# Fourier mixing with a gated MLP: forms made in place, a product begun on a copy, weights split earlier

## The chip, the cores and the metric

The kernel runs on one core of a Trainium2 chip. The metric is the device time of one execution in microseconds. Its engines are TensorE (PE, matrix products, results in PSUM), VectorE (DVE) and ScalarE (ACT, both elementwise), GpSimd (POOL) and SyncE (SP); the last two issue most of the DMA transfers here.

## The reference

Shapes: x is 2048 x 512 (one batch), the sequence matrices are 2048 x 2048, the hidden ones 512 x 512, w1 and w3 are 512 x 1376, w2 is 1376 x 512; all are float32.

```python
a = einsum("bsd,ed->bse", x, dft_hid_re)
b = einsum("bsd,ed->bse", x, dft_hid_im)
y = einsum("ts,bse->bte", dft_seq_re, a) - einsum("ts,bse->bte", dft_seq_im, b)

h = silu(x @ w1) * (x @ w3)
o = h @ w2

g = sigmoid((x * gate_w).sum(-1, keepdims=True))
return g * y + (1 - g) * o
```

## The kernel before, in words

**Arithmetic.** Each float32 operand is split in two: a high half, made by ScalarE's copy into the matrix format (`zh`, `f1P`, `wa` and so on), and a low half, made by VectorE's subtraction of the high half from the source (`split`, lines 70 to 74). One product is then three matmuls (`mm3`, line 81: high with high, high with low, low with high). A 2 x 2 block product is computed by seven block products instead of eight, in the manner of Strassen and Winograd. They are named P1 to P7, and their operands are blocks or sums of blocks ("forms").

**Stages.** First come the hidden-dimension products (14 of them, tiles `dP`), whose results go to the scratch `ab` in HBM. Then eleven items, one for each chunk `c` of 128 columns of w1 and w3 (`item(c)`, products into the banks `X`, `Z`, `Y`, `Yi`), which write h to the scratch `hsp` and `hpl`. Then six blocks 0 to 5: for `m` = 0 (h times w2), 1 (real part) and 2 (imaginary part), and two halves of the rows each. Blocks 0 to 3 go through P1, P5, P6, P3, P7, P2, P4 in this order; blocks 4 and 5 have no P2 of their own, but an inner set of seven smaller products (`Lx`). A product has three steps in blocks 0 and 1 (quarters `q` = 0 to 2, and a short "plain" step after P3, P7, P2 and P4), and four in blocks 2 to 5. `STEPS` lists all the steps, and `AT[b, k, q]` is the number of one of them. Block 0 is steps 0 to 24, block 1 begins at step 25.

**The stationary forms.** `forms(m, q, ks, keep)` loads a quarter of `ab` (two tiles `r`) or of w2, makes the sums that the products in `ks` need (tiles `m..P`), splits each, and either keeps the result in SBUF (`keep` true: in place, a tile of the pool `op`) or stores it in the scratch `fsp` (`keep` false), from where `load_a` fetches it when its block draws near (tiles `a0P`, `a1P`, `a2P`). It returns a list of functions, one for the loads and one for each product. `inner_forms` does the same for the inner set, and its stores go to `lsp`. The functions with `keep` false, and the inner ones, stand in the list `later`; `work(n)` takes `n` of them. Twelve are taken in the hidden stage, and six in each item (hooks `h0` to `h4`). Those with `keep` true stand in `TASKS`, a table of what is done after a given step.

**The moving forms.** For step `n`, `load_c` fetches a raw block up to eight steps ahead (tiles `B`), `sum_c` adds blocks four steps ahead (line 669), and `split_c` splits three steps ahead (tiles `zh` and `zl`, from a pool of eight).

**PSUM.** Four pairs of banks, with the tags 0 to 3. P1 opens pair 1 or 0, P5 pair 2, P2 pair 3; P6, P7 and P4 go on accumulating on P1's, and P3 on P5's. After P1, P5 and P6 ScalarE copies the pair to SBUF (line 906), and VectorE adds the later product to that copy (line 911), after which `finish` scales and stores it. In the items, pairs 0 and 1 are `X`, pair 2 is `Y` and `Yi`, and pair 3 is `Z`.

**What sets the order.** A planner puts the instructions of every engine into a queue of their own at compile time. It follows the order of the program, but takes a later instruction first where, by its own estimate of durations, that one is ready sooner. An instruction passed to `pinned` stays behind what its engine had before it. On the chip each queue runs strictly in the order so made.

**The start of the items.** `begun(0)` lets ScalarE copy `X` into `Y` (line 358), so that `Y` goes on from there. The parts of `second(0, ...)` follow in the order 0, 3, 1, 4, 2, 5, and part 3 is `begun`. After them `prep_wa(1)` splits chunk 1's weights (`wa`, on lines 71 and 74), which item 0 uses in `first1(1)`.

Of the kernel before, what the change touches and what calls it, by code (L numbers as in the profile page):

```python
# [9 lines left out]
AF = mybir.ActivationFunctionType  # L10
# [18 lines left out]
def fnet_swiglu_gate_kernel(  # L29
# [17 lines left out]
    nc = tc.nc  # L47
# [8 lines left out]
    def pair(k, name):  # L56
        return psum.tile([P, 2, 512], F32, tag=f"pp{k}", name=name)

    def raw(name, n=1024):
        return f4.tile([P, n], F32, tag="f4", name=name)  # L60

    def half(ap, n=2):
        return ap.rearrange("p (a n) -> p a n", a=n)

    def flat(ap):
        return ap.rearrange("p a n -> p (a n)")

    pinned = tc.keep_in_program_order

    def split(hi, lo, src, pin=False):  # L70
        i = nc.scalar.activation(hi, src, AF.Copy)  # L71
        if pin:
            pinned(i)
        nc.vector.tensor_sub(lo, src, hi.bitcast(F32))  # L74
# [177 lines left out]
    def prep_wa(c):  # L252
        n = 768 if c == NC - 1 else 512
        if n == 512:
            t = zo.tile([P, 2, n], F32R, tag="zo", name=f"wa{c}")
            h, l = t[:, 0], t[:, 1]
        else:
            h, l = (zo.tile([P, n], F32R, tag="zo", name=f"wa{c}{v}") for v in "hl")
        split(h, l, WS[c][:, :n], c == 1)
        WA[c] = half(h, n // 256), half(l, n // 256)  # L260
# [201 lines left out]
    def rows_of(m, q):  # L462
        if m == 0:
            return [w2[h, q] for h in range(2)]
        return [ab[m - 1, g, q].rearrange("p h i e -> p (h i e)") for g in range(2)]

    def width(m, q):
        return 256 if m == 0 and 2 * q + 1 == NP else 512
# [4 lines left out]
    def forms(m, q, ks, keep):  # L473

        n = width(m, q)
        st = {}

        def load():
            for h, src in enumerate(rows_of(m, q)):
                st[h] = raw(f"r{m}{q}{h}")  # L480
                nc.sync.dma_start(st[h][:, : 2 * n], src[:, : 2 * n])
            st["a11"], st["a21"] = (st[0][:, v * n : (v + 1) * n] for v in range(2))
            st["a12"], st["a22"] = (st[1][:, v * n : (v + 1) * n] for v in range(2))

        def total(k):
            if k in ("P5", "P3") or k == "P7" and "m" not in st:
                st["m"] = raw(f"m{m}{q}{k}")
            if k == "P5":
                src = st["m"][:, :n]
                nc.vector.tensor_sub(src, st["a22"], st["a21"])  # L490
                st["s5"] = src
            elif k == "P6":
                src = st["m"][:, n : 2 * n]
                minus_sum(src, st["s5"], st["a11"])
                st["s6"] = src
            elif k == "P3":
                src = st["m"][:, :n]
                minus_sum(src, st["a12"], st["s6"])
            elif k == "P7":
                src = st["m"][:, n : 2 * n]  # L500
                nc.vector.tensor_sub(src, st["a11"], st["a21"])
            else:
                src = st[{"P1": "a11", "P2": "a12", "P4": "a22"}[k]]
            st[k] = src

        def parts(k):
            src = st[k]
            pool, tag = (op, "op") if keep else (f4, "f4")
            t = pool.tile([P, 2, n], F32R, tag=tag, name=f"f{m}{k}{q}")
            split(t[:, 0], t[:, 1], src)  # L510
            if keep:
                A[m, k, q] = t
            else:
                nc.gpsimd.dma_start(fsp[m, PRODS.index(k), q, :, : 2 * n], flat(t.bitcast(F32)))

        return ahead(load, total, parts, ks)
# [63 lines left out]
    def fetch(o, i):  # L580
        tc.keep_in_program_order(nc.sync.dma_start(o, i))

    def load_a(m, k, q):
        n = width(m, q)
        t = A[m, k, q] = op.tile([P, 2, n], F32R, tag="op", name=f"a{m}{k}{q}")
        fetch(flat(t.bitcast(F32)), fsp[m, PRODS.index(k), q, :, : 2 * n])
# [4 lines left out]
    CHAIN = (("P1", "B11"), ("P5", "F1"), ("P6", "F2"), ("P3", "B22"),  # L591
             ("P7", "F3"), ("P2", "B21"), ("P4", "F4"))
# [3 lines left out]
    LB = (4, 5)  # L596
    FORM = dict(CHAIN)
    INNER = [(k, h) for k in ("P1", "P5", "P6", "P3", "P7", "P4", "P2") for h in range(2)]
    todo = list(INNER)
    STEPS, AT = [], {}  # L600
# [210 lines left out]
    U, BANKS, WHOLE = {}, {}, {}  # L811
# [35 lines left out]
    def step(n):  # L847
        b, k, q, form = STEPS[n]
        m, j = BLOCKS[b]
        if k[0] == "L":  # L850
            if q == 0 and k in ("LP7", "LP2"):
                load_other(LB[k == "LP2"], 0, 0)
            return inner(n)
        end = b == len(BLOCKS) - 1
        if q == 0:
            for f in ACTS.get((b, k), ()):
                f()
            if k in QUARTER:
                load_other(b, *QUARTER[k])
            if k in ("P1", "P5", "P2"):  # L860
                tag = {"P1": (1, 0)[b % 2], "P5": 2, "P2": 1 if end else 3}[k]
                WHOLE[k] = pair(tag, f"{k}_{b}")
                BANKS[k] = [WHOLE[k][:, r] for r in range(2)]
        acc = {"P6": "P1", "P7": "P1", "P4": "P1", "P3": "P5"}.get(k, k)
        ps, whole = BANKS[acc], WHOLE[acc]
        own = k in ("P1", "P5", "P2")
        fin = n == FINAL[b, k]
        zh, zl = ZO.pop(n)
        if q == "pl":
            e = QUARTER[k][0]  # L870
            for r in range(2):
                sl = slice(e * 256 + r * P, e * 256 + (r + 1) * P)
                mm3(ps[r], W2L[0][:, 0, sl], W2L[0][:, 1, sl], zh, zl, False, True, True)
        else:
            w = A[m, k, q]
            todo = [(q, w, zh, zl)]
            if n >= len(STEPS) - 2:
                LASTS.extend(todo)
                todo = LASTS if n == len(STEPS) - 1 else []
                if todo:  # L880
                    ps = [psum.tile([P, 512], F32, tag=f"pp{v}", name=f"last{v}") for v in (2, 3)]
            for r in range(2):
                for qq, ww, h, l in todo:
                    nch = chunks(b, qq)
                    for i in range(nch):
                        a = slice(i * 256 + r * P, i * 256 + (r + 1) * P)
                        c = slice(i * 512, (i + 1) * 512)
                        mm3(ps[r], ww[:, 0, a], ww[:, 1, a], h[:, c], l[:, c],
                            (own and qq == 0 or len(todo) == 2 and qq == todo[0][0]) and i == 0, (qq == NQS[m] - 1 or n == len(STEPS) - 3) and i == nch - 1, True)
                if n == len(STEPS) - 1:  # L890
                    finish(b, *QUARTER[k], U[k, b], ps[r], r)
        advance(n)
        for f in TASKS.pop(n, ()):
            f()
        if n == len(STEPS) - 3:
            U[k, b] = half(raw(f"u{k}_{b}"))
            finish(b, *QUARTER[k], U[k, b], whole)
        if not fin or n == len(STEPS) - 1:
            return
        if (k, b) in U:  # L900
            t = U[k, b]
            nc.vector.tensor_add(t[:, 0], t[:, 0], whole[:, 0])
            nc.scalar.activation(t[:, 1], whole[:, 1], AF.Copy)
        elif k in ("P1", "P5", "P6"):
            t = U[k, b] = half(raw(f"u{k}_{b}"))
            nc.scalar.activation(flat(t), flat(whole), AF.Copy)
        elif k == "P4":
            finish(b, *QUARTER[k], half(raw(f"u{k}_{b}")), whole)
        else:
            t = U[{"P3": "P6", "P7": "P5", "P2": "P1"}[k], b]  # L910
            nc.vector.tensor_add(flat(t), flat(t), flat(whole))  # L911
            finish(b, *QUARTER[k], t)

# [32 lines left out]
    later += prep_w2l()  # L946
    for q in range(3):
        later += forms(2, q, [k for k in PRODS if k != "P2"], False)
    for q in range(3):
        later += forms(1, q, ("P1", "P5", "P6", "P3"), False)  # L950
    later += inner_forms()

# [19 lines left out]
    first1(0)  # L972
    for n in (0, 3, 1, 4, 2, 5):
        second(0, n, 1)
    prep_wa(1)

    A0 = [(k, q) for k, _ in CHAIN for q in range(NQS[0])]
    for c in range(NC):
# [47 lines left out]
    ACTS, TASKS = {}, {}  # L1026
# [15 lines left out]
            TASKS.setdefault(start + 3 * q + max(i - 1, 0), []).append(f)  # L1042
    for i, (k, q) in enumerate(A0[8:]):
        TASKS.setdefault(int(1.25 * i), []).append(lambda k=k, q=q: load_a(0, k, q))
    todo = forms(1, 3, ("P1", "P5", "P6", "P3"), True)
    todo[:2] = [lambda fs=todo[:2]: [f() for f in fs]]
    todo += [lambda k=k, q=q: load_a(1, k, q) for k, _ in CHAIN[:4] for q in range(3)]
    for i, f in enumerate(todo):
        TASKS.setdefault(AT[1, "P1", 0] + 2 + 2 * i, []).append(f)
    todo = forms(2, 3, [k for k in PRODS if k != "P2"], True)  # L1050
    todo[:2] = [lambda fs=todo[:2]: [f() for f in fs]]
    todo += [lambda k=k, q=q: load_a(2, k, q) for k in LORDER for q in range(3)]
# [75 lines left out]
```

## Time and profile before

| | us |
|---|---|
| median of three runs | 704.97 (703.85 to 705.36) |
| the profiled execution, its own time | 703.83 |
| its span (first to last instruction) | 701.9 |
| TensorE busy | 695.6 |
| VectorE busy | 580.3 |
| ScalarE busy | 353.8 |

185.39 MB move by DMA in the span, at 264 GB/s on average. The granted clock of TensorE is full throughout.

Rows of the profile read as follows. A group: line, engine, operation, written tile `<-` read tiles, shape, count, busy time in us, mean ns of one, idle time just before. A wait: who waited, for whom, us in all, times, longest. A row of the timeline: start in us, duration, engine, line, operation, and in brackets the idle time before and what ended it. The chain of work that ended last is told in pieces with their start and length. A row of the table by stretches gives the busy us of each engine (with its instructions), the clock, the share of the DMA engines in use and GB/s. A row of DMA issues gives the count, the size and the median us from issue to landing; a row of one tile gives ns as least, median and most.

### The profile page before, as it was taken

The page shows a single profiled execution, that of the slowest core. Times are in us where ns is not written, and L with a number is a line of the kernel's source. Part 1 is how long each engine was busy: PE and PEld are TensorE (multiplying, and loading weights), DVE is VectorE, ACT ScalarE, POOL GpSimd, SP SyncE. Part 2 cuts the span into 40 slices and gives each one's busy share as a digit, 9 for nine tenths or more (in the row PEclk, how much of TensorE's full clock was granted, in tenths as well). Part 3 has the DMA queues.
Part 4 walks back from the last instruction along what each step waited for, and adds up shares of the span by engine and source line. Part 5 has one row for each costly group of instructions (what it writes and reads, how often), then busy time and mean ns, then how long its engine had stood idle before and what let it go on. Part 6 is the DMA issues. An engine that isn't in the chain of part 4 may idle for free.

```text
span 701.9 us, 8638 instructions
## 1 busy us (share of the span) xinstructions
PE 695.6 (99%) x3061; PEld 573.4 (82%) x3061; DVE 580.3 (83%) x650; ACT 353.8 (50%) x415; POOL 90.9 (13%) x144
## 2 busy tenths in 40 slices
PE   9999999999999999999999999999999999999997
PEld 7888878888888888788888888888888888888886
DVE  6999667597878987679988998679786966999886
ACT  6746356465555455373463464445534444544531
POOL 0012302131212222000000001000000020111110
PEclk9999999999999999999999999999999999999999
DMA  8387945677787989989569869930889979798823
GB/s 299 144 290 296 353 177 212 225 255 298 288 297 267 328 312 384 378 310 403 199 247 404 313 261 234 328 126 31 312 317 357 359 134 288 210 352 245 212 33 88
DMA packets 57451, 185.39 MB, mean 264 GB/s; under 512 B 6140, under 2 KB 6908, under 8 KB 57408
## 3 DMA queue, kind: packets, MB, share of 16 engines
q1 hardware_dynamic: 37008, 114.18, 45.6%
q0 software_dynamic: 20256, 70.53, 30.7%
q8 instruction: 24, 0.39, 0.2%
q14 instruction: 19, 0.16, 0.1%
q10 hardware_dynamic: 144, 0.13, 0.1%
HBM read 122.16 MB, written 62.66 MB: 263 GB/s over the span
## 4 chain that ended last, share of the span: by engine, by line
PE 94%; DMA 3%; DVE 2%; issue 1%; ACT 0%; DVEq 0%; SPq 0%; ACTq 0%
PE P L81 54%; PE X L81 15%; PE dP L81 10%; PE Z L81 7%; PE Lx L81 3%; PE Yi L81 2%; DMA B<-hsp 2%; PE Y L81 1%; PE dP L206 1%; PE last L81 1%; DMA dB<-head 0%; DVE u L439 0%; DVE B L669 0%; DVE s L405 0%; DVE u L435 0%
## 5 line engine op out<-in xcount | busy, mean ns | idle before, releaser
L71 ACT ACTIVATE zh<-B 128x1024 fp32r<-128x1024 f32 x146 | 148.3, 1019 | 176.3 <-PE P L81 145.1
L74 DVE TENSOR_TENSOR zl<-B,zh 128x1024 fp32r<-128x1024 f32 x146 | 169.6, 1169 | 41.2 <-ACT zh L71 36.0
L669 DVE TENSOR_TENSOR B<-B,B 128x1024 f32<-128x1024 f32 (+1 forms) x76 | 87.4, 1162 | 5.2 <-DMA B<-hsp 4.8
L81 PE MATMUL P<-zh,a2P 128*128 128x512 f32 x280 | 89.0, 389 | 0.0
L81 PE MATMUL P<-zh,a0P 128*128 128x512 f32 x280 | 87.5, 389 | 0.0
L81 PE MATMUL P<-zh,f1P 128*128 128x512 f32 x256 | 80.1, 389 | 0.0
L81 PEld LDWEIGHTS P<-zh,a0P 128*128 128x128 f32 x280 | 52.6, 188 | 11.0
L81 PEld LDWEIGHTS P<-zh,a2P 128*128 128x128 f32 x280 | 52.6, 188 | 10.9
L81 PE MATMUL P<-zh,a1P 128*128 128x512 f32 x192 | 60.4, 389 | 0.0
L81 PEld LDWEIGHTS P<-zh,f1P 128*128 128x128 f32 x256 | 48.0, 188 | 10.0
L81 PE MATMUL P<-zl,a0P 128*128 128x512 f32 x140 | 54.6, 390 | 0.7 <-DVE zl L74 0.7
L81 PE MATMUL P<-zl,a2P 128*128 128x512 f32 x140 | 54.5, 389 | 0.0
L81 PE MATMUL P<-zl,f1P 128*128 128x512 f32 x128 | 49.8, 389 | 0.0
L81 PEld LDWEIGHTS P<-zh,a1P 128*128 128x128 f32 x192 | 36.0, 188 | 7.6
L81 PE MATMUL P<-zl,a1P 128*128 128x512 f32 x96 | 37.3, 389 | 0.0
L81 PEld LDWEIGHTS P<-zl,a0P 128*128 128x128 f32 x140 | 26.3, 188 | 6.4 <-DVE zl L74 1.1
L81 PEld LDWEIGHTS P<-zl,a2P 128*128 128x128 f32 x140 | 26.3, 188 | 5.5
L81 PE MATMUL P<-zh,f2P 128*128 128x512 f32 x88 | 28.9, 389 | 0.0
L81 PEld LDWEIGHTS P<-zl,f1P 128*128 128x128 f32 x128 | 24.0, 188 | 5.0
L71 ACT ACTIVATE zh<-LB 128x1024 fp32r<-128x1024 f32 x14 | 14.9, 1063 | 20.4 <-PE P L81 18.2
L911 DVE TENSOR_TENSOR uP<-uP,P 128x1024 f32<-128x1024 f32 x16 | 19.5, 1219 | 4.4 <-PE P L81 4.3
L81 PEld LDWEIGHTS P<-zl,a1P 128*128 128x128 f32 x96 | 18.0, 188 | 3.7
(1137 smaller groups left out, 1476.0 us busy)
## 6 DMA issues: line engine op xcount, KB each, us to landing
B<-cc SPq DMA_DIRECT2D x56, 512.0 KB, 6.8
r<-ab SPq DMA_DIRECT2D x24, 512.0 KB, 6.3
hsp<-u POOLq DMA_DIRECT2D x20, 512.0 KB, 5.2
fsp<-f2P POOLq DMA_DIRECT2D x18, 512.0 KB, 4.0
a2P<-fsp SPq DMA_DIRECT2D x18, 512.0 KB, 7.2
B<-hsp SPq DMA_DIRECT2D x16, 512.0 KB, 10.4
fsp<-f0P POOLq DMA_DIRECT2D x14, 512.0 KB, 4.3
a0P<-fsp SPq DMA_DIRECT2D x14, 512.0 KB, 11.3
```

What stands on the lines that cost most here:

```text
L71: i = nc.scalar.activation(hi, src, AF.Copy)
L74: nc.vector.tensor_sub(lo, src, hi.bitcast(F32))
L81: nc.tensor.matmul(ps, u, v, start=first and n == 0, stop=last and n == 2, skip_group_check=chain)
L206: tc.keep_in_program_order(nc.tensor.matmul(ps[j][:, i], u[:, 0, sl], v[:, 0], start=start, stop=False, skip_group_check=True))
L669: nc.vector.tensor_add(t, t, RAW[b, o, q])
L911: nc.vector.tensor_add(flat(t), flat(t), flat(whole))
```

## The change

It has four parts.

- **P2 on a copy of P1.** In blocks 0 to 3 ScalarE's copy of P1 goes to PSUM pair 3 instead of SBUF, pinned, and P2's matmuls accumulate on it. VectorE no longer adds P2 to P1; `finish` reads the pair itself. For blocks 0 and 1 that is VectorE's scaling, which now reads PSUM, and for blocks 2 and 3 it is a copy by ScalarE.
- **Quarter 2 of `forms(1)`, in place.** P1, P5, P6 and P3 of that quarter leave the list `later` (five functions, four stores to `fsp`) and the fetches of `a1P` (four of twelve), and are made with `keep` true.
- **Places in `TASKS`.** Quarter 3, made in place already, moves from steps 27 to 33 (block 1) to steps 6 to 12 (block 0). Quarter 2 takes steps 27 to 33. The eight fetches of `a1P` that are left take every second step from 35 to 49; before, twelve took those from 35 to 57.
- **`prep_wa(1)`** stands behind part 3 of `second(0, ...)`, which is second of six, and no longer behind all of them.

```diff
@@ step
-            if k in ("P1", "P5", "P2"):
-                tag = {"P1": (1, 0)[b % 2], "P5": 2, "P2": 1 if end else 3}[k]
+            if k in ("P1", "P5"):
+                tag = {"P1": (1, 0)[b % 2], "P5": 2}[k]
                 WHOLE[k] = pair(tag, f"{k}_{b}")
                 BANKS[k] = [WHOLE[k][:, r] for r in range(2)]
...
-        own = k in ("P1", "P5", "P2")
+        own = k in ("P1", "P5")
...
+        elif k == "P1" and b not in LB:
+
+            WHOLE["P2"] = pair(3, f"P2_{b}")
+            BANKS["P2"] = [WHOLE["P2"][:, r] for r in range(2)]
+            pinned(nc.scalar.activation(flat(WHOLE["P2"]), flat(whole), AF.Copy))
         elif k in ("P1", "P5", "P6"):
             t = U[k, b] = half(raw(f"u{k}_{b}"))
             nc.scalar.activation(flat(t), flat(whole), AF.Copy)
-        elif k == "P4":
+        elif k in ("P2", "P4"):
             finish(b, *QUARTER[k], half(raw(f"u{k}_{b}")), whole)
         else:
-            t = U[{"P3": "P6", "P7": "P5", "P2": "P1"}[k], b]
+            t = U[{"P3": "P6", "P7": "P5"}[k], b]
             nc.vector.tensor_add(flat(t), flat(t), flat(whole))
             finish(b, *QUARTER[k], t)
@@ the list later
-    for q in range(3):
+    for q in range(2):
         later += forms(1, q, ("P1", "P5", "P6", "P3"), False)
@@ before the items
     for n in (0, 3, 1, 4, 2, 5):
         second(0, n, 1)
-    prep_wa(1)
+        if n == 3:
+            prep_wa(1)
@@ TASKS
-    todo = forms(1, 3, ("P1", "P5", "P6", "P3"), True)
-    todo[:2] = [lambda fs=todo[:2]: [f() for f in fs]]
-    todo += [lambda k=k, q=q: load_a(1, k, q) for k, _ in CHAIN[:4] for q in range(3)]
+    todo = []
+    for q in (3, 2):
+        fs = forms(1, q, ("P1", "P5", "P6", "P3"), True)
+        todo += [lambda fs=fs[:2]: [f() for f in fs]] + fs[2:]
+    todo += [lambda k=k, q=q: load_a(1, k, q) for k, _ in CHAIN[:4] for q in range(2)]
     for i, f in enumerate(todo):
-        TASKS.setdefault(AT[1, "P1", 0] + 2 + 2 * i, []).append(f)
+        TASKS.setdefault(AT[0, "P6", 0] + 2 * i if i < 4 else AT[1, "P1", 0] + 2 * i - 6, []).append(f)
```

## The prediction

> **What bounds the kernel now.** I read the page's totals first, then TensorE's own waits, then the chain in order of time.
>
> ```profile
> span 701.9 us, 8638 instructions
> PE 695.6 (99%) x3061; PEld 573.4 (82%) x3061; DVE 580.3 (83%) x650; ACT 353.8 (50%) x415; POOL 90.9 (13%) x144
> PE P L81 <- DVE zl L74: 0.7, 1, 0.7
> PE X L81 <- ACT wa L71: 0.3, 1, 0.3
> 273.93 15.41 DMA B<-hsp
> 296.49 284.31 PE P L81 x1253
> ```
>
> TensorE bounds nearly the whole span. The change neither adds nor removes a matmul, so it can gain only what TensorE loses in waits. Behind the head, which is not touched, the view of TensorE's waits has only these two (`X <- wa`, `P <- zl`), and both are where the change works. The chain's long row gives the pace: 284.31/1253 = 0.227 us from one matmul to the next. With it I measure what each wait really costs, since a busy TensorE also runs late just behind a wait.
>
> The first place is the start of item 0, where `first1(1)` needs the split weights of chunk 1:
>
> ```profile
> 94.30 0.39 PE L81 MATMUL Z<-x1F3h,wb0l 128*128 128x512 f32 x1
> 95.02 0.50 PE L81 MATMUL X<-x0B11h,wa 128*128 128x512 f32 x1 [0.34 <-ACT wa L71]
> 95.36 0.39 PE L81 MATMUL X<-x0B11l,wa 128*128 128x512 f32 x1
> 95.75 0.73 PE L81 MATMUL X<-x0B11h,wa 128*128 128x512 f32 x2
> 96.32 0.40 PE L81 MATMUL X<-x0B11l,wa 128*128 128x512 f32 x1
> ```
>
> From 94.30 to 96.32 lie five steps (one row holds two): 2.02 us where the pace gives 1.13. Lost: 0.89 us.
>
> The second place is block 0, at the first low half of its second product (P5):
>
> ```profile
> 295.22 0.61 PE L81 MATMUL P<-zh,a0P 128*128 128x512 f32 x2
> 296.49 0.50 PE L81 MATMUL P<-zl,a0P 128*128 128x512 f32 x1 [0.66 <-DVE zl L74]
> 296.83 0.63 PE L81 MATMUL P<-zh,a0P 128*128 128x512 f32 x2
> 283.47 1.22 DVE L435 TENSOR_TENSOR u<-u,X 128x1024 f32<-128x1024 f32 x1 [2.08 <-PE X L81]
> 289.47 1.23 DVE L669 TENSOR_TENSOR B<-B,B 128x1024 f32<-128x1024 f32 x1 [4.78 <-DMA B<-hsp]
> 295.22 1.22 DVE L74 TENSOR_TENSOR zl<-B,zh 128x1024 fp32r<-128x1024 f32 x1
> 288.66 1.06 ACT L71 ACTIVATE zh<-B 128x1024 fp32r<-128x1024 f32 x1 [2.14 <-PE X L81]
> ```
>
> From 295.22 to 296.83 lie three steps: 1.61 us instead of 0.68, so 0.93 lost. The row that matters is not the late `zl` (its `zh` was there at 289.72) but the sum at 289.47. VectorE stood 4.78 us before it, for the load that the chain shows as 15.41 us long (273.93 to about 289.35), and everything behind it slid.
>
> Together 0.89 + 0.93 = 1.82 us, 0.26% of the run. What a measurement of this kernel can tell from no change is about 0.2%, here 1.41 us.
>
> **The change, part by part.** *Weights of chunk 1 sooner (`prep_wa(1)`).*
>
> ```profile
> 86.62 1.03 ACT L358 ACTIVATE Y<-X 128x1024 f32<-128x1024 f32 x1
> 88.47 0.60 ACT L391 ACTIVATE s<-Yi 128x512 f32<-128x512 f32 x1 [0.83 <-PE Yi L81]
> 94.36 0.61 ACT L71 ACTIVATE wa<-ws 128x512 fp32r<-128x512 f32 x1
> 89.10 0.69 DVE L392 TENSOR_TENSOR s<-s,Yi 128x512 f32<-128x512 f32 x1 [4.75 <-ACT s L391]
> 95.00 0.69 DVE L74 TENSOR_TENSOR wa<-ws,wa 128x512 fp32r<-128x512 f32 x1 [1.70 <-ACT wa L71]
> ```
>
> Nothing is added; one ScalarE step (0.61) and one VectorE step (0.69) move. The split is now queued behind L358 (the copy that opens `Y`), which ends at 87.65, and ScalarE stands 0.83 us there before L391: 0.61 fits, 87.6 to 88.2. The low half follows at 88.3 to 89.0 inside VectorE's 4.75 us of idle time. Both are then ready some 5 us before 94.52, when the pace would want them. If the cover were gone, L391 would slip by at most 0.4 us. The next thing late at 94.52 is nothing that I can find: the raw chunk is loaded and the bank emptied before item 0 begins. Gain 0.89, bounds 0.5 to 0.9.
>
> *Quarter 2 of `forms(1)` made in place.* This takes five tasks out of the list that items 0 to 10 work off, hence four stores of `fsp`, two loads of `r` and four later loads of `a1P`.
>
> ```profile
> r<-ab SPq DMA_DIRECT2D x24, 512.0 KB, 6.3
> fsp<-f1P POOLq DMA_DIRECT2D x12, 512.0 KB, 5.0
> L572 POOL DMA_DIRECT2D lsp<-flP x7: 534/543/562, 255.7 to 275.4; - x7
> 255.00:276.00 21.00, 21.00 (x95) 17.38 (x94) 16.50 (x24) 11.69 (x15) 6.53 (x11) 1.00 0.99 363
> 276.00:290.00 14.00, 14.00 (x63) 11.59 (x62) 7.14 (x7) 5.46 (x7) 0.72 (x1) 1.00 1.00 400
> ```
>
> The transfers are full from 255 to 290 (shares 0.99 and 1.00), and the seven `lsp` stores of the inner forms lie in that stretch. Each item works off six tasks, so with five fewer ahead they come almost one item, some 15 to 18 us, sooner: the last at about 258. Six of them (3.1 MB) started before the load of 273.93; at 400 GB/s that is 7.9 us of transfers ahead of it, so it should land near 281.5 instead of 289.35. VectorE is free for its sum at 283.47 + 1.22 = 284.7: the 4.78 us go. What is late next is the `zh` of 288.66, which waits for TensorE itself: `zl` can end at 291.0, some 4.6 us before it is wanted. Even half the relief would do, since the `zl` misses by only 0.8 us. Gain 0.93, bounds 0 to 0.93.
>
> *Quarter 3 sooner (block 0, steps 6 to 12), quarter 2 in its old place (block 1).* A quarter is seven VectorE steps (four low halves, three sums) and four on ScalarE, and block 0 gets them new:
>
> ```profile
> L74 DVE TENSOR_TENSOR f1P<-r,f1P x12: 681/684/691, 209.5 to 426.6; 128x512 fp32r<-128x512 f32 x12
> L71 ACT ACTIVATE f1P<-r x12: 613/617/622, 208.8 to 425.4; 128x512 fp32r<-128x512 f32 x12
> 303.00:318.00 15.00, 15.00 (x68) 12.43 (x67) 9.70 (x12) 12.33 (x14) 1.13 (x2) 1.00 1.01 366
> 342.00:362.00 20.00, 20.00 (x90) 16.57 (x89) 20.00 (x25) 11.36 (x15) 0.72 (x1) 1.00 0.39 138
> ```
>
> That is 7 x 0.684 = 4.8 us of VectorE and 4 x 0.617 = 2.5 us of ScalarE. Steps 6 to 12 run at 303 to 318, where VectorE is busy 9.70 of 15.00 and ScalarE 12.33: 5.3 and 2.7 us are free, enough but with little over. Block 1, where VectorE is at 20.00 of 20.00, exchanges one quarter for another of the same size. I price this at 0 and give the load of `r`, which now meets full transfers (1.01), to the second rival. It could also gain nothing: TensorE waits nowhere from 297 on.
>
> *P2 accumulated on ScalarE's copy of P1, four blocks.*
>
> ```profile
> L358 ACT ACTIVATE Y<-X x6: 1007/1008/1030, 86.6 to 264.4; 128x1024 f32<-128x1024 f32 x6
> L906 ACT ACTIVATE uP<-P x17: 1007/1009/1030, 300.9 to 663.2; 128x1024 f32<-128x1024 f32 x17
> L911 DVE TENSOR_TENSOR uP<-uP,P x16: 1212/1221/1222, 320.0 to 686.9; 128x1024 f32<-128x1024 f32 x16
> ```
>
> The copy of P1 goes into PSUM instead of SBUF: the same copy, L358 against L906, takes 1008 against 1009 ns. Four VectorE sums (1.22 each, 4.9 in all) go; in blocks 2 and 3 two ScalarE copies of P2 (L906's 1.01 each) take their place. A tile of the pool `f4` is free from P1 to P2. All of this is off TensorE's path, since the bank that P2 starts on is filled some 25 us before. Value 0; at worst P6 waits for the pinned copy, which in block 0 stood at 300.90 and was needed at 303, and is now queued sooner.
>
> **A rule against the rows.** The rows: 0.227 us per matmul over 1253 of them, and 12.33 of 15.00 or 20.00 of 20.00 us on the other engines beside them without a wait. The Trainium skill, page "TensorE: Matmul & The Clock Gate", section "Wait — 56ns, not 53.3ns?", gives about 215.7 ns from start to start for 512 columns at full clock. By that page of the Trainium skill an estimated 11 ns lie open in each matmul, 14 us in the chain's long row, which lighter traffic might win back; the run would then come to about 691. The trace does not agree: the stretches 303–318 and 342–362 have transfer shares of 1.01 and 0.39 and the same pace within one matmul (68 in 15.00, 90 in 20.00, counting those cut at the edges). So the sum keeps 0.227, and that case gets no chance of its own.
>
> **Sum.** The profiled execution took 703.83 us (span 701.9 and 1.9 around it): 703.83 - 1.82 = 702.0. It lies 1.14 below the median of the runs, 704.97, so the median becomes 704.97 - 1.82 = 703.15; I say 703.1.
>
> **Rivals.** *Only the weights' wait goes.* The planner that orders VectorE's queue may put another sum ahead of the splits, or the load may still come late. For it: the order rests on estimated landings, and 15.41 us was not foreseen. Against it: nearly 8 us of stores leave its way. 704.97 - 0.89 = 704.1: no change that can be told.
>
> *ScalarE waits for `r` in block 0 (slower).* The loads of `r` are issued at step 6, into full transfers:
>
> ```profile
> a0P<-fsp SPq DMA_DIRECT2D x5, 512.0 KB, 11.5
> 302.73 1.64 SPq L581 DMA_DIRECT2D a0P<-fsp  x3
> 331.32 1.21 SPq L481 DMA_DIRECT2D r<-ab  x2
> 346.30 0.61 ACT L71 ACTIVATE f1P<-r 128x512 fp32r<-128x512 f32 x1
> 312.50 0.62 PE L81 MATMUL P<-zh,a0P 128*128 128x512 f32 x2
> ```
>
> Issued beside the `a0P` of 302.73 and with their 11.5 us, `r` lands at about 314.5. If the first split of quarter 3 then stands ahead of step 10's `zh` in ScalarE's queue, that `zh` and its `zl` end at 314.5 + 0.6 + 1.06 + 1.22 = 317.4; TensorE wants them at about 312.95 (the matmul after the pair of 312.50). That costs 4.4 us, net 2.6: 707.5. It begins to cost from a landing after 310.1, and makes the kernel slower by over 0.2% from 313.3 on. Against it: before, the loads ran 15 us ahead of their split (331.32, 346.30), and with 3 MB fewer transfers before 300 (8 us at 400 GB/s) the queue is not so deep. By the Trainium skill, page "TensorE: Matmul & The Clock Gate", section "What's actually happening", an idle window of about 3.4 us halves the clock for about as long; an estimated 1.7 us more would come on top, and no run here shows such a drop.
>
> *Nothing gained.* The planner leaves the split where it was, or the waits are replaced by equal ones: 705.0.
>
> **How the numbers follow.** Both waits go and nothing new comes: 0.50, around 703.1, between 702.0 (if the slower runs of before had lost more than the profiled one to the late load) and 703.9. Only the weights: 0.18. `r`: 0.24. Nothing: 0.08. Faster by over 0.2% (below 703.56): 0.45 of the first case. Same: the remaining 0.05, 0.18, 0.08 and 0.02 of `r`, 0.33. Slower: 0.22. Range 701.8 to 707.0, which leaves out the worse half of the `r` case and a little below; the likeliest case alone spans 702.0 to 703.9.
>
> **What would show it.** Right: `X <- wa` gone from TensorE's waits and the split near 88 on ScalarE; the last `lsp` store before 262; VectorE's wait for `B<-hsp` under 1 us and no `P <- zl`; L911 with 12 instead of 16; 3061 matmuls at 0.227. Wrong: a ScalarE row `f1P <- DMA r<-ab` near 305 to 315, or any TensorE wait past 300 of over 1 us.

## The result, and the profile after

| | before | after |
|---|---|---|
| median, 22 runs each, us | 704.88 | 703.09 |
| lowest to highest, us | 703.20 to 706.36 | 701.74 to 704.94 |
| the profiled execution, its own time, us | 703.83 | 704.94 |

The ratio is 0.9971, with a 95% interval of 0.9963 to 0.9979: faster by 1.8 us going by the medians and by 2.0 us going by the ratio (1.5 to 2.6). Two executions among those of the experiments below, 1601.57 us in e7 and 1433.38 us of the kernel before beside e1 to e4, took over twice as long as the rest and are left out of the ratios. The profiled execution of after happens to be the longest of its 22 runs; that has to be understood before the two traces are compared.

The totals of the page after, and then two rows of its groups by line:

```profile
span 702.8 us, 8615 instructions
PE 695.0 (99%) x3061; PEld 573.2 (82%) x3061; DVE 575.6 (82%) x646; ACT 355.8 (51%) x417; POOL 88.5 (13%) x140
```

```profile
L916 DVE TENSOR_TENSOR uP<-uP,P 128x1024 f32<-128x1024 f32 x12 | 14.6, 1217 | 3.1 <-PE P L81 3.1
L669 DVE TENSOR_TENSOR B<-B,B 128x1024 f32<-128x1024 f32 (+1 forms) x76 | 87.6, 1164 | 0.4
```

The additions to a copy, line 911 before, now stand on line 916, twelve instead of sixteen. The sums of line 669 no longer wait for a transfer (0.4 us of idle time where it was 5.2, 4.8 of them for `B<-hsp`).

TensorE's waits after, all of them:

```profile
PE Z L81 <- ACT dt1P L226: 1.4, 1, 1.4
PE Yi L81 <- DVE s L392: 1.3, 1, 1.3
PE wps L929 <- PEq L1126: 0.8, 1, 0.8
PE dP L206 <- ACT dB21h L132: 0.4, 1, 0.4
```

Both waits that the prediction worked with (`X <- wa`, `P <- zl`) are gone. The last two rows are the start of the run (its first 5 us), which was there before. The first two are new, and they make the profiled execution long. The timeline after, with the matmuls on both sides of each and what came ahead of it:

```profile
81.30 0.69 DVE L490 TENSOR_TENSOR m01P<-r,r 128x512 f32<-128x512 f32 x1 [2.25 <-DMA r<-w]
85.00 0.39 PE L81 MATMUL Yi<-bth,wp0f 128*128 128x512 f32 x1
86.81 0.50 PE L81 MATMUL Z<-x0F3h,wb0h 128*128 128x512 f32 x1 [1.42 <-ACT dt1P L226]
87.14 0.39 PE L81 MATMUL Z<-x0F3l,wb0h 128*128 128x512 f32 x1
230.84 0.43 DVE L266 TENSOR_TENSOR wu<-ws 128x256 f32<-128x256 f32 x1 [4.51 <-DMA fsp<-f1P]
232.40 0.39 PE L81 MATMUL X<-x1F1h,wb7l 128*128 128x512 f32 x1
234.12 0.50 PE L81 MATMUL Yi<-x1B21h,wp4zo 128*128 128x512 f32 x1 [1.34 <-DVE s L392]
234.46 0.40 PE L81 MATMUL Yi<-x1B21l,wp4zo 128*128 128x512 f32 x1
```

Two steps from 85.00 to 87.14 take 2.14 us where the pace gives 0.45, and two from 232.40 to 234.46 take 2.06: 1.69 + 1.61 = 3.30 us lost. VectorE stands behind a load at 81.30 and behind a store at 230.84. The chain of waits after gives both transfers, and the pace:

```profile
71.79 9.42 DMA r<-w
222.17 8.64 DMA fsp<-f1P
290.88 291.04 PE P L81 x1284
```

Before, the same two took 8.1 and 7.0 us, and VectorE went on at 79.53 and 228.68. The change moves no instruction across them, and it doesn't decide alone whether they come. The experiment with only the second product changed (e3 below), where nothing before block 0 differs from the kernel before, has the wait at 85 too (1.45 us). The experiment with the whole change and block 0's sums put in order (e9) has neither (VectorE at 79.20 and 228.22). So these two come and go with how long transfers take in one execution. An estimate of the profiled execution without them, if nothing behind them had waited instead, is 704.94 - 3.30 = 701.6 us, beside the 702.0 of the prediction's sum.

The places where the change works, in the timeline after:

```profile
88.54 0.65 ACT L71 ACTIVATE wa<-ws 128x512 fp32r<-128x512 f32 x1
89.22 0.69 DVE L74 TENSOR_TENSOR wa<-ws,wa 128x512 fp32r<-128x512 f32 x1 [3.09 <-ACT wa L71]
286.67 2.36 DVE L669 TENSOR_TENSOR B<-B,B 128x1024 f32<-128x1024 f32 x2
315.06 0.62 ACT L71 ACTIVATE f1P<-r 128x512 fp32r<-128x512 f32 x1
```

The split of chunk 1 stands at 88.54 instead of 94.36. Block 0's sums at 286.67 start with no wait. The first split of quarter 3 in block 0 (315.06) waits for nothing either. The inner stores, and the three loads of `B<-hsp` issued between 270 and 290, in the views of one tile (ns of one issue as least, median and most in the first two rows, us from issue to landing in the last):

```profile
L572 POOL DMA_DIRECT2D lsp<-flP x7: 532/541/562, 240.9 to 261.3; - x7
L581 SPq DMA_DIRECT2D B<-hsp x3: 333/384/482, 275.2 to 286.6; - x3
DMA to landing us min/median/max: 2.7/9.0/10.9
```

Before, the seven stores ran from 255.7 to 275.4, and the three loads took 3.5, 13.1 and 15.4 us.

### The profile page after: what moved, and what is told of

It is laid out like the page before. It is cut to its first block, busy times and chain, and to the rows that moved or that the text cites. A ratio compares the mean times of both kernels' runs of the same rounds, so it can differ in the third digit from the quotient of the medians.

```text
span 702.8 us, 8615 instructions
## 1 busy us (share of the span) xinstructions
PE 695.0 (99%) x3061; PEld 573.2 (82%) x3061; DVE 575.6 (82%) x646; ACT 355.8 (51%) x417; POOL 88.5 (13%) x140
## 2 busy tenths in 40 slices
DMA packets 56299, 181.20 MB, mean 258 GB/s; under 512 B 6012, under 2 KB 6780, under 8 KB 56256
## 4 chain that ended last, share of the span: by engine, by line
PE 84%; issue 6%; DMA 4%; DVE 3%; POOL 2%; ACT 0%; SPq 0%; DVEq 0%; POOLq 0%; ACTq 0%
PE P L81 55%; PE X L81 12%; PE Z L81 6%; PE dP L81 5%; PE Lx L81 3%; PE Yi L81 1%; DMA r<-w 1%; DMA fsp<-f1P 1%; PE Y L81 1%; PE dP L206 1%; POOL fsp L514 1%; DMA ab<-dt1P 1%; PE last L81 1%; POOL hsp L411 0%; DMA dB<-head 0%
## 5 line engine op out<-in xcount | busy, mean ns | idle before, releaser
L81 PE MATMUL P<-zh,f1P 128*128 128x512 f32 x320 | 99.9, 389 | 0.0
L81 PEld LDWEIGHTS P<-zh,f1P 128*128 128x128 f32 x320 | 60.0, 188 | 12.4
L81 PE MATMUL P<-zl,f1P 128*128 128x512 f32 x160 | 62.2, 389 | 0.0
L81 PEld LDWEIGHTS P<-zh,a2P 128*128 128x128 f32 x280 | 52.6, 188 | 10.9
L81 PE MATMUL P<-zh,a1P 128*128 128x512 f32 x128 | 40.7, 389 | 0.0
L81 PEld LDWEIGHTS P<-zl,f1P 128*128 128x128 f32 x160 | 30.1, 188 | 6.3
L81 PEld LDWEIGHTS P<-zh,a1P 128*128 128x128 f32 x128 | 24.0, 188 | 5.0
L81 PE MATMUL P<-zl,a1P 128*128 128x512 f32 x64 | 24.9, 389 | 0.0
L435 DVE TENSOR_TENSOR u<-u,X 128x1024 f32<-128x1024 f32 x11 | 13.4, 1217 | 10.6 <-PE X L81 10.3
L74 DVE TENSOR_TENSOR zl<-LB,zh 128x1024 fp32r<-128x1024 f32 x14 | 17.1, 1220 | 4.4 <-ACT zh L71 4.4
```

What stands on the lines that cost most here:

```text
L81: nc.tensor.matmul(ps, u, v, start=first and n == 0, stop=last and n == 2, skip_group_check=chain)
L435: nc.vector.tensor_add(u4, u4, flat(x))
```

## The experiments

Each was timed beside the kernel before on the same chip (its medians 704.85 for e1 to e4, 704.65 for e5 to e8, 704.33 for e9 to e12). Ratios are to it.

**e1: only the weights sooner.** Kernel before, and:

```diff
     for n in (0, 3, 1, 4, 2, 5):
         second(0, n, 1)
-    prep_wa(1)
+        if n == 3:
+            prep_wa(1)
```

> The kernel before with only the split of chunk 1's weights moved forward. By the theory of the prediction TensorE's wait X <- wa near 94 us goes and 0.89 us with it (ratio 0.9987), while block 0 keeps its wait P <- zl near 295 us with about 0.9 us. By the rival that the gain comes from the lighter transfers alone, the time stays (1.0000). By the rival that the moved split delays the copies behind it on ScalarE, a wait of up to 0.4 us on Yi takes its place.

704.62 us, ratio 1.0002 (0.9984 to 1.0019). `X <- wa` is gone. The interval holds 1.0000 and the expected 0.9987 alike, so the times don't tell whether the edit gains anything alone. The timeline of e1 at the second place:

```profile
290.06 1.23 DVE L669 TENSOR_TENSOR B<-B,B 128x1024 f32<-128x1024 f32 x1 [5.56 <-DMA B<-hsp]
295.02 0.61 PE L81 MATMUL P<-zh,a0P 128*128 128x512 f32 x2
297.08 0.50 PE L81 MATMUL P<-zl,a0P 128*128 128x512 f32 x1 [1.45 <-DVE zl L74]
297.42 0.62 PE L81 MATMUL P<-zh,a0P 128*128 128x512 f32 x2
```

Three steps from 295.02 to 297.42 take 2.40 us instead of 0.68: 1.72 lost, where it was 0.93. Of the 0.79 us more, 0.20 are that TensorE comes to this place sooner (295.02 instead of 295.22), and 0.59 that the sum starts later (290.06 instead of 289.47), behind a load that is 16.3 us long here and was 15.4. So this trace doesn't show that what is won upstream is only waited for here.

A wait on `Yi`, the third case that was expected, is there with 0.16 us at 231.83, but e2 and e4, whose weights are split where they were before, have it too (0.32 us at 233.39, 0.36 at 232.85).

Other traces speak against waits that don't add up. In the profiled execution of e3, which has the wait at 85, TensorE comes to block 0's first matmul at 290.94 instead of 288.64, 2.30 us later than before, and still it waits 0.57 us at this place, nearly the 0.66 of before. The chain of e3 has the same load:

```profile
275.83 15.72 DMA B<-hsp
```

It was issued 1.90 us later than before (275.83, 273.93), so the end of the wait moved with TensorE. In the six executions whose transfers come late as before (before, e1, e3 to e6) this load is issued between 14.5 and 15.2 us ahead of that first matmul, which itself comes anywhere from 288.45 to 290.94.

**e2: only the forms** (the edits of `later` and of `TASKS`).

```diff
-    for q in range(3):
+    for q in range(2):
         later += forms(1, q, ("P1", "P5", "P6", "P3"), False)
... and the edits of TASKS, as in the change
```

> The kernel before with only quarter 2 made in place, quarter 3 made sooner and the fetches of a1P moved with them. By the theory VectorE's wait of 4.78 us for B<-hsp near 289 us goes, with it P <- zl near 295 us, 0.93 us in all (ratio 0.9987); X <- wa near 94 us stays with about 0.9 us. By the rival that the late load comes from something else, both stay and the time is as before. By the rival of the prediction ScalarE waits over 2 us for r<-ab near 305 to 315 us and the kernel is slower by up to 0.4%.

703.81 us, ratio 0.9988 (0.9976 to 1.0000). `P <- zl` is gone, `X <- wa` is there as before (0.3 us), and the longest of the three loads takes 10.8 us. The gain of 0.12%, 0.85 us, agrees with the 0.93 of the second place, though the interval just reaches no gain.

**e3: only the second product on ScalarE's copy** (the edits of `step`).

```diff
+        elif k == "P1" and b not in LB:
+            WHOLE["P2"] = pair(3, f"P2_{b}")
...
+            pinned(nc.scalar.activation(flat(WHOLE["P2"]), flat(whole), AF.Copy))
```

> The kernel before with only P2 accumulated on ScalarE's copy of P1. By the theory nothing on TensorE's path changes: both waits stay and the ratio is 1.000 within 0.001; VectorE's busy time falls by about 4.9 us (four sums of 1.22), ScalarE's rises by about 2. By the rival that the relief of VectorE or the free tile is what the change gains by, the ratio is near 0.997 and P <- zl is gone.

704.59 us, ratio 1.0006 (0.9991 to 1.0022): no gain that can be told. Both waits stay (`P <- zl` 0.6, `X <- wa` 0.3 us).

**e4: only the order.** Kernel before, with block 0's three sums of P7 kept where the program has them:

```diff
-        nc.vector.tensor_add(t, t, RAW[b, o, q])
+        i = nc.vector.tensor_add(t, t, RAW[b, o, q])
+        if b == 0 and form == "F3":
+            pinned(i)
```

> The kernel before with block 0's three sums B12+B22 kept behind what the program has before them on VectorE, and no transfer changed. By the theory it is this sum, queued ahead of the splits though not needed until P7, that turns the late load into TensorE's wait: the load of B<-hsp still takes about 15 us, but VectorE does not wait for it before the low halves of steps 2 and 3, P <- zl near 295 us goes and the ratio is 0.9987. By the rival that the transfers are late for the splits themselves, VectorE waits 2 us or more at the next sum (B11+B22), P <- zl stays or moves to step 6, and the ratio is 1.000.

703.56 us, ratio 0.9982 (0.9971 to 0.9993). No transfer was changed, and the loads are as late as before; still `P <- zl` is gone. The three loads of e4, and VectorE's timeline:

```profile
DMA to landing us min/median/max: 3.1/13.5/15.1
```

```profile
290.56 1.23 DVE L74 TENSOR_TENSOR zl<-B,zh 128x1024 fp32r<-128x1024 f32 x1
291.82 1.22 DVE L669 TENSOR_TENSOR B<-B,B 128x1024 f32<-128x1024 f32 x1
309.73 1.22 DVE L669 TENSOR_TENSOR B<-B,B 128x1024 f32<-128x1024 f32 x1
```

VectorE comes to the `zl` of 290.56 without standing for a load. The sum that stood at 289.47 ahead of the splits, one of P7's three, is now far behind them, at 309.73, with the other two at 313.54 and 315.81. The sum of 291.82 is one that P6 needs; it has no wait either, since the slowest of the three loads, issued at 274.96, landed near 290.06. So the late load does no harm by itself; what hurt was that the planner had put a sum needed only by P7 ahead of the splits for P5, on a queue that runs in order.

**e5: the weights and the order** (the edits of e1 and e4, nothing else).

> The kernel before with the weights of chunk 1 split sooner and block 0's three sums B12+B22 kept in program order on VectorE; no transfer, form or product changed. By the theory that both waits are single places which the two small edits remove, this gives as much as the whole change: ratio 0.997, neither X <- wa nor P <- zl on TensorE. By the rival that the four forms made in place and the lighter transfers have a worth of their own, it stays at 0.9985 or above.

702.73 us, ratio 0.9970 (0.9959 to 0.9980). All of TensorE's waits of e5:

```profile
PE wps L926 <- PEq L1121: 0.8, 1, 0.8
PE Yi L81 <- DVE s L392: 0.2, 1, 0.2
```

Two small edits of order give as much as the change, within the intervals. No worth of its fewer transfers, its forms in place or its second product beside that can be told from these times.

**e6: only quarter 3 sooner** (into block 0, quarter 2 as before).

```diff
-        TASKS.setdefault(AT[1, "P1", 0] + 2 + 2 * i, []).append(f)
+        TASKS.setdefault(AT[0, "P6", 0] + 2 * i if i < 4 else AT[1, "P1", 0] + 2 + 2 * i, []).append(f)
```

> The kernel before with quarter 3 of forms(1) made at steps 6 to 12 and nothing else: its two loads of r now come in block 0, without the lighter transfers before them. By the theory of the prediction's slower rival ScalarE waits for r<-ab near 305 to 315 us and TensorE with it (2 to 4 us, ratio 1.002 to 1.006). By the theory that the load runs ahead of its split anyway, TensorE has no wait past 300 us and the ratio is 1.000, with P <- zl near 295 us as before.

704.35 us, ratio 1.0002 (0.9990 to 1.0013): no cost, and no wait of TensorE past 300 us. The two loads of `r` there take 8.2 and 9.7 us, and ScalarE's split at 314.18 has no wait for them: the `zh` of 308.85 and 312.28 and the gate's work stand ahead of it.

**e7: the change with the order fixed, and two tasks fewer in the hidden stage** (a try to gain both ways).

```diff
-        nc.vector.tensor_add(t, t, RAW[b, o, q])
+        i = nc.vector.tensor_add(t, t, RAW[b, o, q])
+        if b == 0 and form == "F3":
+            pinned(i)
...
-        if 7 <= n < 13:
+        if 7 <= n < 12:
             work(2)
```

> The changed kernel with the three sums kept in order, and with two of the twelve tasks of the hidden stage left to the items (those of its last product, whose sum on VectorE waited for a load of r and held ScalarE's copy of dP, 1.6 us of TensorE at 85 us in the changed kernel's profile). By the theory this wait goes in every run: the median falls by up to 1.3 us against the changed kernel (about 702, ratio 0.995 to before). By the rival that such a wait comes in few runs or only moves, the median is that of the changed kernel (703.1).

706.62 us, ratio 1.0031 (1.0019 to 1.0042): slower. Two new waits of TensorE, `X <- ACT g` at 224 us (one step of 2.27 us) and `P <- zl` at 320 (1.26 us). e9 and e10 take them apart.

**e8: e7 with five tasks in each item instead of six.**

```diff
 in hook h4
-            work(2)
+            work(1)
```

> The same, with five tasks in each item instead of six, so that the 55 left fill all eleven items. By the theory the wait at 232 us of the changed kernel's profile (VectorE's sum for chunk 8 waits for a store of f1P to release its tile, 1.5 us of TensorE) goes too, since fewer stores are under way at once: ratio 0.993 to 0.995. The inner stores come late again, so by the rival that late stores harm block 0 even with the sums in order, a wait P <- zl near 295 us returns and the ratio is 0.997 or above.

708.82 us, ratio 1.0062 (1.0048 to 1.0076). Late transfers hold up ScalarE in block 0, as in the prediction's slower rival, but `r` is the smaller part. The timeline of e8 in block 0, by engines, and after it the table by stretches (length; busy us of each engine; the granted clock, share of the DMA engines and GB/s last):

```profile
312.57 1.28 ACT L745 ACT_TABLE_LOAD   x1 [2.73 <-DMA gt<-gs]
316.97 0.63 ACT L71 ACTIVATE f1P<-r 128x512 fp32r<-128x512 f32 x1 [0.58 <-DMA r<-ab]
320.93 2.00 ACT L71 ACTIVATE zh<-B 128x1024 fp32r<-128x1024 f32 x2 [1.29 <-DVE B L669]
319.62 1.22 DVE L669 TENSOR_TENSOR B<-B,B 128x1024 f32<-128x1024 f32 x1
317.39 1.52 PE L81 MATMUL P<-zp,w2lh 128*128 128x512 f32 x6
322.04 0.49 PE L81 MATMUL P<-zh,a0P 128*128 128x512 f32 x1 [3.13 <-ACT zh L71]
323.30 0.50 PE L81 MATMUL P<-zl,a0P 128*128 128x512 f32 x1 [0.77 <-DVE zl L74]
324.10 0.48 PE L81 MATMUL P<-zl,a0P 128*128 128x512 f32 x1
327.75 0.40 PE L81 MATMUL P<-zl,a0P 128*128 128x512 f32 x1
```

```profile
324.40:327.40 3.00, 3.00 (x9) 2.35 (x8) 3.00 (x6) 1.66 (x3) 0.00 (x0) 0.50 1.04 414
```

With fewer tasks taken in the items the transfers slide into block 0. ScalarE stands 2.73 us for `gt` (the scores of the gate) and 0.58 for `r`. Then the `zh` that TensorE needs waits 1.29 us for a sum on VectorE (319.62), one of the three for P7, which the fixed order keeps behind the first forms of quarter 3; without that order (after, e10) no sum stands on VectorE between 306 and 325. By the pace the last of the six matmuls of 317.39 starts near 318.52, so the two steps that end at 322.04 and 323.30 take 3.52 and 1.26 us: 4.33 lost. Of these, 1.03 us is what the fixed order costs in e9 with no late load. Then the granted clock is 0.50, and the nine steps from 324.10 to 327.75 take 3.65 us instead of 2.04: 1.6 more.

**e9: the change with the order fixed, nothing else** (e7 without the edit of the hidden stage).

> The changed kernel with one thing more: block 0's three sums of its last product are kept behind the sums of the second product's halves. Theory A (the order of VectorE's queue and the transfers are two ways to the same 0.9 us, and in a kernel that forms quarter 3 in block 0 the fixed order puts those three sums behind forms that wait for r): the wait P<-zl of about 0.8 to 1.3 us that the kernel with order and fewer tasks had at 320 us is here too, the ratio to the kernel before is 0.998 to 1.000, worse than the change alone (0.9971). Theory B (that wait came from the task count, not from the order): no wait past 300 us, ratio 0.996 to 0.9975, the same as the change alone or a little better.

703.30 us, ratio 0.9986 (0.9973 to 0.9998). Theory A: the wait at 320 belongs to the order. The timeline of e9:

```profile
314.33 1.22 DVE L669 TENSOR_TENSOR B<-B,B 128x1024 f32<-128x1024 f32 x1
316.74 1.22 DVE L74 TENSOR_TENSOR zl<-B,zh 128x1024 fp32r<-128x1024 f32 x1
316.76 0.49 PE L81 MATMUL P<-zh,a0P 128*128 128x512 f32 x1
318.02 0.50 PE L81 MATMUL P<-zl,a0P 128*128 128x512 f32 x1 [0.76 <-DVE zl L74]
```

The sums now follow the forms of quarter 3 in block 0, and the splits for P7 miss by 0.76 us. The step takes 1.26 us, 1.03 lost, and 0.9986 against 0.9971 is 1.06 us. The two intervals overlap, so the time alone would not settle it; the row does.

**e10: the change with two tasks fewer in the hidden stage** (`n < 12` alone).

> The changed kernel with one planned step fewer in which hidden tasks are issued (steps 7 to 11 instead of 7 to 12). Theory A (the step of 2.26 us at 224 us, X<-ACT g, in the kernel with order and fewer tasks came from the tasks that slid behind): that wait is here too, about 2 us, the wait at 320 us is not, ratio 0.9985 to 1.000. Theory B (the task count is free): ratio 0.9965 to 0.9978, as the change alone.

704.92 us, ratio 1.0009 (0.9999 to 1.0020). Theory A again for the wait: the one at 224 belongs to the tasks, which slide into the items; the ratio lies just above the range that theory A gave. The profiled execution is the longest of the twelve (707.60; the others 704.08 to 705.61). The timeline of e10, and a stretch of its table:

```profile
224.59 0.39 PE L81 MATMUL Yi<-bth,wp4f 128*128 128x512 f32 x1
227.11 0.50 PE L81 MATMUL X<-x0B11h,wa 128*128 128x512 f32 x1 [2.12 <-ACT g L451]
227.44 0.42 PE L81 MATMUL X<-x0B11l,wa 128*128 128x512 f32 x1
231.07 0.40 PE L81 MATMUL X<-x1B11l,wa 128*128 128x512 f32 x1
```

```profile
227.60:231.00 3.40, 3.40 (x10) 2.67 (x9) 0.71 (x1) 2.26 (x4) 0.84 (x2) 0.51 0.81 288
```

2.29 us are lost to the wait (2.52 less one step), and again the clock falls to half behind it: nine steps from 227.44 to 231.07 take 3.63 us, 1.6 too many. The fall is this execution's: its mean clock is 0.998, which is what 3.4 us at half clock take from a mean over 705.6 us, and that of the other eleven is 0.999 or 1.00.

**e11: the change without the second product's edits** (e1 and e2 together).

> The weights and the four forms together, the second product left as it was (added to the first product's copy by VectorE). Theory A (the product's edit is worth nothing; the gain is the two others together, each alone gives 0 to 0.1%): ratio 0.9965 to 0.9978, neither X<-wa nor P<-zl, and the sums of the kind L911 stay at 16. Theory B (the 4 us of VectorE that the product's edit frees are needed to keep P<-zl away): P<-zl of 0.4 us or more, ratio 0.9985 to 0.9995.

702.57 us, ratio 0.9974 (0.9964 to 0.9984): the same as the whole change, within the intervals. Neither wait is there, and sixteen sums stand on line 911. In its profile TensorE waits 0.9 us at 86.62, in the place of the 1.42 us of after.

**e12: a candidate.** The edits of e5, quarter 2 in place, and both quarters formed in block 1:

```diff
-        TASKS.setdefault(AT[1, "P1", 0] + 2 + 2 * i, []).append(f)
+        TASKS.setdefault(AT[1, "P1", 0] + 2 + (2 * i if i < 8 else i + 8), []).append(f)
```

> A candidate: the weights sooner, block 0's three sums kept in order, quarter 2 formed in place, and both quarter 3 and quarter 2 formed in block 1 (none in block 0); the second product as before. Theory A (what costs is a form that waits for r in block 0; block 1 has room): neither of the two waits, no wait of ScalarE for r near 305 to 315 us, ratio 0.996 to 0.9972. Theory B (block 1 has no room: VectorE is busy all of 342 to 362 us there): a wait of TensorE of over 0.5 us between 340 and 400 us, ratio 0.998 to 1.001.

706.06 us, ratio 1.0016 (1.0005 to 1.0027): slower, as theory B has it, but with the wait at 419 us, outside the stretch that theory B named. The timeline of e12, and the stretch ahead of the wait:

```profile
415.57 1.06 ACT L71 ACTIVATE zh<-B 128x1024 fp32r<-128x1024 f32 x1 [2.72 <-DVE B L669]
418.19 1.01 ACT L908 ACTIVATE uP<-P 128x1024 f32<-128x1024 f32 x1
419.24 0.50 PE L81 MATMUL P<-zh,a1P 128*128 128x512 f32 x1 [1.88 <-ACT uP L908]
```

```profile
394.00:417.00 23.00, 23.00 (x104) 19.01 (x102) 21.26 (x21) 10.09 (x12) 0.56 (x1) 1.00 0.76 299
```

`zh` waits 2.72 us for a sum on VectorE, and the copy of a finished bank stands behind that `zh`. That VectorE is full doesn't explain it: it is busy 21.26 of 23 us here, and 22.96 in the same stretch of the kernel before, which has no wait. There the two sums together stand at 409.15 on VectorE and here at 414.24, behind forms that both kernels have; why they stand later was not tested. The edit also puts the fetches of `a1P` closer together (steps 43 to 50), so it changes more than the place of the forms. No version tried beats the change by more than can be told; e5 and e11 equal it.

## Why the prediction came out as it did

The total was right, 703.1 against 703.09, and so was the mechanism, TensorE's two waits: the versions without either and with no new wait in block 0 (after, e5, e11) lie at 0.9970 to 0.9974, those that keep one or both (e1 to e4, e6) at 0.9982 to 1.0006. That the total agrees to 0.01 us is luck, since the interval of the gain is 1.1 us wide. Step by step:

- **Weights, 0.89 us.** Right that the split moves near 88 and that the wait goes; it landed at 88.54, since the execution was already late. What the edit is worth alone stays open: the interval of e1 (-0.16% to +0.19%) holds nothing and the 0.89 us alike. With the second wait out of the way it is worth about its price: e5 against e4 (0.9970, 0.9982) is 0.85 us, and e11 against e2 (0.9974, 0.9988) is 0.99 us, though the intervals of each pair overlap. The prediction added the two waits without asking what ends the second. The traces under e1 say that the sum was right: the load that ends it is issued with TensorE's arrival. The rival "only the weights' wait goes", priced at 704.1, did not come, since both went.
- **Quarter 2 in place, 0.93 us.** The stores came 14.1 us sooner (last at 261.3; 15 to 18 was forecast). The relief of the load was sized too large: 7.9 us was forecast, and the longest of the three loads took 10.9 us instead of 15.4, 4.5 less. That was enough, as the prediction allowed for: the sums started at 286.67 without a wait, and e2 gives 0.85 us. What the prediction did not see is that the load need not have been faster at all. It called the sum at 289.47 the row that matters, which is right, but it did not ask who needed that sum: only P7, many steps later. e4 takes the sum out of the way and leaves the load at 15.1 us, and the wait goes all the same.
- **Quarter 3 in block 0, priced 0.** Right (e6: 1.0002). In the profile after, the `r` took 7.6 and 8.2 us instead of the 11.5 that the rival assumed, and the split at 315.06 found it there.
- **Second product on the copy, priced 0.** Right within the intervals (e3: 1.0006; e11 without it: 0.9974). The sums fall to twelve.
- **Pace kept at 0.227.** Right: 291.04/1284 = 0.2267 us, with 181.20 MB moved instead of 185.39. The lighter traffic won back 0.2 ns a matmul of the 11 ns that lie between this and the 215.7 ns of the Trainium skill's page "TensorE: Matmul & The Clock Gate", section "Wait — 56ns, not 53.3ns?".
- **The slower rival**, 4.4 us for a late `r` and 1.7 us for the clock, did not come here. It let a landing after 310.1 cost, on the condition that the first split of quarter 3 stands ahead of a `zh` that TensorE is about to need. In e6 the two loads, issued at 304.8 and 305.3, land no sooner than 313.0, where the rival's sum has 2.9 us of cost; TensorE doesn't wait, and the split stands at 314.18. By the planner's order the condition doesn't hold there. In e8 4.33 and 1.6 us were lost, close to both prices. For the first that is luck: ScalarE's wait for `r` is 0.58 us, beside 2.73 for `gt` and the fixed order of P7's sums, and the rival names neither. The price of the clock was right.
- **What was not foreseen** are the two waits of the profiled execution after, 3.30 us together. "A TensorE wait past 300 of over 1 us" was the sign that the prediction gave for being wrong. None came there; these came earlier, and in other kernels too.

Open stays why the same transfer takes 8.1 us in one execution and 9.42 in another; the traces show that it does, not why.

## What to carry to other kernels

Before adding up waits on one path, ask of each whether its end moves when the engine comes sooner: if it does, they add, and if it doesn't, what is won before it is only waited for later. A wait that ends with a transfer can be of either kind; here the transfer was issued with the engine's arrival (e3), and a timing with an interval wider than the gain (e1) could not have told. Where an engine stands before an instruction whose load is late, look first whether that instruction is needed there; here putting three sums in order (0.9982) was worth as much as moving 3 MB of transfers out of the way (0.9988), within the intervals. And try a fix of order again in every version: the one that helps the old kernel put a wait that costs 1 us into the changed one, whose forms stood in between.

## What the hardware showed that was not expected

**Half clock after a short stall.** In e10 TensorE waited 2.12 us at 227.11, and some 0.5 us after it went on its granted clock fell to 0.51 for 3.4 us. In e8 it waited 3.13 and 0.77 us, with 0.50 after it. Waits of 1.42 and 1.34 us (after) and of 1.88 us (e7 and e12) left it at 1.00. Each drop cost 1.6 us on top of the wait. It doesn't come in every execution of a kernel: of e10's twelve the profiled one alone has a mean clock below 0.999, and of e12's twelve five others have 0.996 where the profiled one has 0.999. No trace shows where it fell in those. The Trainium skill, page "TensorE: Matmul & The Clock Gate", section "What's actually happening", has the clock halve after an idle window of about 3.4 us, and recover after about 3.4 us of work. The length of the drop agrees; the 2.12 us of e10 are shorter than that window, and here the measurement decides: a wait of 2.12 us can be enough.

**The same transfer, from one execution to the next.** A load of `r` issued near 72 us took 8.1 us before and 9.42 after, and a store issued near 222 us took 7.0 and 8.64. In after both were also issued some 0.5 us later than before. With VectorE's queue standing behind each, 1.3 and 1.6 us more on a transfer went with 1.69 and 1.61 us of TensorE's time, each nearly as much as the whole change is worth.
